# The second mixing one step later, a third buffer of mixed blocks, and the weight conversion spread over more steps

## The chip, the cores and the metric

The kernel runs on one core of a Trainium2 chip. The metric is the device time of one execution in microseconds (us), from start to end of the program. The profiler shows five engines: TensorE (PE, with its weight loads in a row of their own, PEld), VectorE (DVE), ScalarE (ACT), GpSimd (POOL) and SyncE (SP), which here issues DMAs.

## What is computed

Talking-heads attention (4 batches, 12 heads, 448 positions, 64 values a head), then a two-layer network on the result. Two 12x12 matrices mix the heads, one before and one after the softmax:

```python
scores = scale * np.matmul(q, k.transpose(0, 1, 3, 2))
scores = np.einsum('bhij,hg->bgij', scores, w_pre)
scores = scores - np.max(scores, axis=-1, keepdims=True)
attn = np.exp(scores)
attn = attn / (np.sum(attn, axis=-1, keepdims=True) + 1e-09)
attn = np.einsum('bhij,hg->bgij', attn, w_post)
out = np.matmul(attn, v).astype(np.float32)
...
h = x @ w_in
r = np.maximum(h, 0.0)
g = s * (r * r) + b
return (g @ w_out).astype(np.float32)
```

## The kernel before, in words

Precision is kept with pairs: a float32 value is split into a high and a low part, and a product takes three matmuls (low by high, high by low, high by high).

**Attention.** The query positions of a batch are cut into four chunks of 110, 110, 110 and 118 (`chunks`, 16 in all). For a chunk, `qk_pair` computes the scores of two heads (six matmuls, line 489) into the two PSUM banks of tag `sc`, and ScalarE copies them to `S` (line 499). DMAs lay `S` out again as blocks of ten positions by twelve heads on 120 partitions (`relayout`). There are 180 blocks: 11 to a chunk of 110, 12 to a chunk of 118. The main loop takes one block a step, in a software pipeline written out by hand. In step s, in this order:

- `split(s + 2)`: GpSimd splits a block into high and low (lines 563, 564);
- one operation of a weight conversion on VectorE (`convert_step`, steps 12 to 60), then `normalize(s - 1)`: reciprocal on VectorE (line 597) and the scaled block `eh` in float16 on ScalarE (line 599);
- `evacuate(s - 3)`: VectorE copies a mixed block from PSUM to `A` (line 637; in the last chunk ScalarE does it, line 635);
- `premix(s)`: the first mixing, three matmuls of 448 columns (line 578), the maximum on VectorE (line 580), the exponential and its sum on ScalarE (lines 585, 589). The result lies in one of three PSUM banks in turn;
- `remainder(s - 1)`: VectorE makes the float16 remainder of the normalized block into the second half of `eh` (line 606);
- `postmix(s - 2)`: the second mixing, twelve matmuls of 120 columns that load `eh` as weights (line 621), into one of two banks of tag `po`;
- what the plan gives the step: the scores of a later chunk (`qk_pair`), the product with V for an earlier one (`av_pair`, line 517, two heads, sixteen matmuls), transposes of q (`prep_q`, `trq`) and of k (`prep_k`, `trk`) into the `sc` banks, whose low parts VectorE makes at the next call of `low_parts` (line 232).

Each engine works through its own list in order. About every second step is given a `qk_pair` and an `av_pair` at once (steps 1, 3, 5, 7, 9 and the last of a chunk's window); the text calls these heavy, the others light. In a window of 11 steps the last two heavy ones adjoin; in one of 12 none do. ScalarE copies the products with V out of PSUM, `xs` (line 531), one or two copies after the fourth and after the sixth `av_pair` of a chunk (two in a chunk of 118).

The plan (`at`, `fill`, `run_plan`) is a list of step numbers. An `av_pair` of a chunk may begin at `first[ci + 1] + 3`, a step after the chunk's last block has been copied to `A`.

**Weight conversion.** The network's weights come as 64-bit floats. `conversion` turns one piece into a high and a low part by one ScalarE operation (line 153) and seven VectorE operations (lines 154 to 177); each call of `convert_step` does one VectorE operation of it. Seven pieces (`NU_EARLY`), 49 operations, are done during the attention, one a step from `CONV0 = 12`.

**Network.** From about 486 us on, two matrix products fill TensorE; the first pieces of the first (`head_piece`) are put into the attention's last steps as filling.

`keep` is a constant tile that feeds matmuls without use in the first steps (line 576), which only keep TensorE at work.

Of the kernel before, what the change touches and what calls it, by code (L numbers as in the profile page):

```python
# [11 lines left out]
F16 = mybir.dt.float16  # L12
# [9 lines left out]
def talking_heads_attention__then__act_relu2_kernel(  # L22
# [14 lines left out]
    B, H, S, D = q.shape  # L37
    DM = H * D
    DFF = moe_w_in.shape[1]
    P = 128  # L40
# [5 lines left out]
    NP = H // 2  # L46
    BI = 10
    BP = BI * H
# [13 lines left out]
    NCH = len(chunks)  # L62
# [3 lines left out]
    first = []  # L66
# [9 lines left out]
    NB = len(blocks)  # L76

    NU = 16
    NU_EARLY, NU_TAIL = 7, 6
# [6 lines left out]
    cvp = ctx.enter_context(tc.tile_pool(name="cvp", bufs=1))  # L86

    att = ExitStack()
    cst = att.enter_context(tc.tile_pool(name="cst", bufs=1))
    sp = att.enter_context(tc.tile_pool(name="sp", bufs=2))  # L90
    blkp = att.enter_context(tc.tile_pool(name="blkp", bufs=3))
# [90 lines left out]
    def convert_step(upto):  # L182

        if done["run"] is None:
            if done["conv"] >= min(upto, len(units)):
                return False
            done["run"] = conversion(done["conv"])
        try:
            next(done["run"])
        except StopIteration:  # L190
            done["run"] = None
            done["conv"] += 1
        return True
# [33 lines left out]
    later = []  # L227
# [4 lines left out]
            nc.vector.tensor_tensor(out=o, in0=x, in1=hi.bitcast(F32), op=ALU.subtract)  # L232

    banks = ["pm", "po", "pm", "po", "xp", "px"]
    turn = {"bank": 0}

    def bank(name):
        tag = banks[turn["bank"] % len(banks)]
# [301 lines left out]
    def qk_pair(ci, p):  # L540
        low_parts()
        for m in range(3):
            qk_part(ci, p, m)
# [7 lines left out]
    def relayout(t):  # L551
        ci, i0, ni = blocks[t]
        blk = blkp.tile([BP, S], F32, tag="blk", name=f"blk_{t}", bufs=LD)
        nb = first[ci + 1] - first[ci]
        r = t - first[ci]
        nc.sync.dma_start(blk[:ni * H, :], s_t[ci][r:r + nb * (ni - 1) + 1:nb, :, :])
        blk_t[t] = blk

    def split(t):
        n = blocks[t][2] * H  # L560
        blk = blk_t.pop(t)
        hl = blkp.tile([BP, 2, S], F32R, tag="hl", name=f"hl_{t}", bufs=2)
        nc.gpsimd.tensor_scalar(hl[:n, 0, :], blk[:n], 1.0, 0.0, op0=ALU.mult, op1=ALU.add)  # L563
        nc.gpsimd.tensor_tensor(  # L564
            out=hl[:n, 1, :], in0=blk[:n], in1=hl[:n, 0, :].bitcast(F32), op=ALU.subtract
        )
        hl_t[t] = hl
# [25 lines left out]
    def normalize(t):  # L593

        n = blocks[t][2] * H
        e, st = e_t[t]
        nc.vector.reciprocal(st[:n, 3:4], st[:n, 2:3])  # L597
        eh = blkp.tile([BP, 2, S], F16, tag="eh", name=f"eh_{t}", bufs=2)
        nc.scalar.activation(eh[:n, 0, :], e[:n], AF.Copy, scale=st[:n, 3:4])  # L599
        eh_t[t] = eh  # L600

# [9 lines left out]
    def postmix(t):  # L611
        ci, i0, ni = blocks[t]
        n = ni * H
        eh = eh_t.pop(t)
        if i0 == 0:
            a_t[ci] = ap_.tile([P, NC, H, CH], F32, tag="A", name=f"A_{ci}")
        po = ps.tile([P, 512], F32, tag="po", name=f"po_{t}", bufs=2)
        for c in range(NC):
            j0 = min(c * P, S - P)
            for m, (x, y) in enumerate(((1, 0), (0, 1), (0, 0))):  # L620
                nc.tensor.matmul(  # L621
                    po[:, c * BP:(c + 1) * BP],
                    eh[:n, x, j0:j0 + P],
                    wpost[:n, y].rearrange("p g i -> p (g i)"),
                    start=(m == 0),
                    stop=(m == 2),
                )
        po_t[t] = po

    def evacuate(t):  # L630
        ci, i0, ni = blocks[t]
        dst = a_t[ci][:, :, :, i0:i0 + ni]
        src = po_t.pop(t)[:, :NC * BP].rearrange("p (c g i) -> p c g i", c=NC, g=H)[:, :, :, :ni]
        if ci == NCH - 1:
            nc.scalar.activation(dst, src, AF.Copy)
        else:
            nc.vector.tensor_copy(dst, src)  # L637

    LD, LS = 5, 2
    CONV0 = 12  # L640
    FILL = 1.33
# [8 lines left out]
    def at(step, order, f, *args):  # L650
        plan.append((step, order, len(plan), f, args))
# [6 lines left out]
    def visits(ci):  # L658

        w0, w1 = first[ci - 1] - LD, first[ci] - LD  # L660
        return [w0 + i for i in (1, 3, 5, 7, 9, w1 - w0 - 1)]

    fill = []
    for ci in range(2, NCH):
        b, _, _ = chunks[ci]
        w0 = first[ci - 1] - LD
# [10 lines left out]
        for p, step in enumerate(visits(ci)):  # L677
            if news:
                t = w0 - back + 8 if p == 0 else w0 + 2 * p - 2
# [4 lines left out]
            load[step] = load.get(step, 0) + QK_COST  # L684
    for ci in range(NCH):
        b = chunks[ci][0]
        w0 = first[ci + 1] + 3
        if ci < NCH - 2:
            after = visits(ci + 3) if ci + 3 < NCH else [first[NCH - 1] - LD + i for i in (1, 3, 5, 7)]
            steps = [x for x in visits(ci + 2) if x >= w0] + [x for x in after if x < first[ci + 2] + 3]  # L690
            assert len(steps) == NP
            for p, step in enumerate(steps):
                at(step, 2, av_pair, ci, p)
                load[step] = load.get(step, 0) + AV_COST
                if b + 1 < B and chunks[ci + 1][0] != b:
                    at(step, 4, load_v, b + 1, p)
            continue
        w1 = first[ci + 2] + 3 if ci + 2 <= NCH else NB + 100
        if ci == NCH - 1:
            w0 = NB + 3  # L700
        for p in range(NP):
            when = w0 + p * min(w1 - w0, 12) / NP
            fill.append((when, w0, w1 - 1, AV_COST, 1, av_pair, (ci, p)))
    w0 = first[NCH - 1] - XA + 2
    for i in range(NHEAD * NKC):
        if i < NHEAD * NKC - LATE:
            j = i - (NHEAD * NKC - LATE - 4)
            if j < 0:
                when = w0 + i * (NB - 1 - w0) / (NHEAD * NKC - LATE - 4)
                fill.append((when, w0 + i // 2, NB + 2, 0.567, 1, head_piece, ()))  # L710
            else:
                at(NB - 1 + (0, 1, 1, 2)[j], 1, head_piece)
        else:
            fill.append((NB + 100, NB + 3, NB + 100, 0.567, 1, head_piece, ()))
    fill.sort(key=lambda x: x[0])
    spent, closed = 0.0, {}
    for s in range(NB + 4):
        spent = max(spent, -0.4) + load.get(s, 0)
        left, held = [], set()
        for x in fill:  # L720
            _, lo, hi, cost, order, f, args = x
            waits = f in held

            opens = f is qk_pair or (f is av_pair and args[1] % 4 == 0)
            if opens and closed.get(f, -1) >= s and s <= NB + 2 and s < hi:
                waits = True

            if f is qk_pair and s in load and s < hi:
                waits = True
            if not waits and lo <= s and (s > NB + 2 or hi <= s or (x[0] < s + 4 and spent < FILL)):  # L730
                at(s, order, f, *args)
                spent += cost
                if f is qk_pair or (f is av_pair and args[1] in (3, NP - 1)):
                    closed[f] = s
            else:
                held.add(f)
                left.append(x)
        fill = left
        spent -= FILL
# [12 lines left out]
        if not early:  # L752
            state["next"] = k0

    keep = cst.tile([P, 512], F16, name="keep")
    nc.gpsimd.memset(keep, 1.0)
    make_identity(nc, ident)
    busy = ps.tile([P, 512], F32, tag="px", name="busy")
# [51 lines left out]
    while plan[0][0] < 0:  # L810
        x = plan.pop(0)
        x[3](*x[4])
        low_parts()
    tail = first[NCH - 1]
    for s in range(NB + 3):
        if s == tail - LD:
            early.close()
            rp = ctx.enter_context(tc.tile_pool(name="rp", bufs=1, side="right", reuse_waits="tile"))
            for n in range(NU_EARLY, NU_EARLY + NU_TAIL):
                w_pool[n] = rp  # L820
        if s + LD < NB:
            relayout(s + LD)
        if s + LS < NB:
            split(s + LS)
        if 0 <= s - 1 < NB:
            if s >= CONV0:
                convert_step(NU_EARLY)
            normalize(s - 1)
        if 0 <= s - 3 < NB:
            evacuate(s - 3)  # L830
        if s <= tail - XA:
            low_parts()
        if s < NB:
            premix(s)
        low_parts()
        if s < 2:
            (build_scale, build_post)[s](*loaded_consts)
            qk_pair(1, NP - 2 + s)
        if 0 <= s - 1 < NB:
            remainder(s - 1)  # L840
        run_plan(s, True)
        if 0 <= s - 2 < NB:
            postmix(s - 2)
        run_plan(s, False)
        if 0 <= s - (tail - LD) < NKC // 2:
            for kc in range(2):
                load_x(0, 0, 2 * (s - (tail - LD)) + kc)
        if 0 <= s - (tail - XA) < NKC:
            split_x(0, 0, s - (tail - XA))
        if 0 <= s - tail < NKC:  # L850
            load_x(0, 1, s - tail)
# [107 lines left out]
```

## Time and profile before

| | |
|---|---|
| median of 3 executions | 961.35 us (959.28 to 961.48) |
| the profiled execution | 961.09 us, span in the trace 959.4 us |
| PE busy over the span | 929.8 us, 97% |
| PEld / DVE / ACT / POOL busy | 82% / 67% / 62% / 41% |
| chain that ended last, by engine | PE 64%, ACT 15%, DVE 13%, DMA 5% |
| granted TensorE clock | 1.00 of full speed (2.4 GHz) in nearly every slice |

A row of the waits names the engine that waited, the line that it waited in, the releaser, the time in total, how often and the longest. A row of the timeline gives start and duration in us, the engine, line and operation, and in brackets the idle time before it with its releaser. Matmuls are pipelined and their ends are modelled, so that a matmul's row can cover a part of the idle time behind it.

### The profile page before, as it was taken

To read this page: it belongs to the slowest core of one execution; us is meant where nothing else is said; L and a number is where in the kernel's file an instruction comes from. 1 tells how busy PE (TensorE), PEld (TensorE's weight loads), DVE (VectorE), ACT (ScalarE), POOL (GpSimd) and SP (SyncE) were. 2 spreads that over 40 slices of the span, in tenths; PEclk is the share of its full clock that TensorE was granted. 3 is DMA by queue.
4 is the path that set the end of the run, shared out by engine and by line. 5 is a ranking of instruction groups with operands and counts; after the bars stand their busy time and mean duration, and the time that the engine had idled before them with its cause. 6 is when DMAs were issued, how large, how long until landed. Compare 5 with 4: busy or idle time off the path is not lost.

```text
span 959.4 us, 19910 instructions
## 1 busy us (share of the span) xinstructions
PE 929.8 (97%) x7538; PEld 786.2 (82%) x7538; DVE 639.0 (67%) x1307; ACT 597.7 (62%) x1321; POOL 398.1 (41%) x469
## 2 busy tenths in 40 slices
PE   8899999999999999999999999999999999999998
PEld 4566767777777777777789999999998999999998
DVE  3899999888878888788678217656707711848311
ACT  5678778787888888877777977322216787711000
POOL 3866676666767667766613423100001332310000
PEclk9999999999999999999999999999999999999999
DMA  4665545654455544645323312245431410237431
GB/s 114 173 155 154 151 126 146 180 129 151 106 147 143 135 118 127 157 116 168 112 71 106 109 55 70 66 126 154 132 133 45 154 58 1 82 110 209 145 98 50
DMA packets 124252, 114.63 MB, mean 119 GB/s; under 512 B 61656, under 2 KB 120044, under 8 KB 124156
## 3 DMA queue, kind: packets, MB, share of 16 engines
q1 hardware_dynamic: 114630, 101.69, 38.3%
q10 hardware_dynamic: 9366, 11.59, 3.4%
q8 instruction: 59, 0.97, 0.4%
q14 instruction: 37, 0.30, 0.1%
q0 software_dynamic: 160, 0.09, 0.1%
HBM read 58.28 MB, written 16.52 MB: 78 GB/s over the span
## 4 chain that ended last, share of the span: by engine, by line
PE 64%; ACT 15%; DVE 13%; DMA 5%; issue 2%; POOL 0%; SPq 0%; ACTq 0%; DVEq 0%
PE po L300 24%; PE ph L247 17%; PE xp L517 6%; PE po L621 5%; ACT S L499 5%; PE sc L489 5%; PE pm L578 5%; ACT pm L585 4%; ACT eh L599 3%; DVE eh L606 3%; DVE A L637 2%; DVE st L580 2%; DMA raw<-in_moe_w_out_dram 2%; DMA nq<-in_q_dram 1%; PE trk L442 1%
## 5 line engine op out<-in xcount | busy, mean ns | idle before, releaser
L300 PE MATMUL po<-w,g 128*128 128x384 f32 x1344 | 234.6, 336 | 2.4 <-ACT h L255 2.4
L300 PEld LDWEIGHTS po<-w,g 128*128 128x128 f32 x1344 | 233.7, 188 | 3.1 <-ACT h L255 3.1
L564 POOL TENSOR_TENSOR hl<-blk,hl 120x448 fp32r<-120x448 f32 x180 | 206.0, 1145 | 15.0
L265 POOL TENSOR_TENSOR g<-h,g 128x448 fp32r<-128x448 f32 x64 | 77.9, 1217 | 287.9 <-ACT g L264 274.8
L621 PEld LDWEIGHTS <-eh 120*128 120x128 f16 (+1 forms) x2160 | 115.0, 98 | 63.4 <-DVE eh L606 40.5
L247 PE MATMUL ph<-x,w 128*128 128x448 f32 x810 | 166.2, 364 | 0.0
L247 PEld LDWEIGHTS ph<-x,w 128*128 128x128 f32 x810 | 152.0, 188 | 12.2
L563 POOL TENSOR_SCALAR hl<-blk 120x448 fp32r<-120x448 f32 x180 | 105.1, 584 | 136.2 <-PE pm L578 123.1
L621 PE MATMUL po<-wpost,eh 120*128 120x120 f16 (+1 forms) x2160 | 144.7, 217 | 14.6 <-DVE eh L606 14.1
L585 ACT ACTIVATE pm<-pm,st 120x448 f32<-120x448 f32 x180 | 109.8, 610 | 56.8 <-DVE st L580 56.2
L606 DVE SCALAR_TENSOR_TENSOR eh<-pm,st,eh 120x448 f16<-120x448 f32 x180 | 122.1, 679 | 16.6 <-ACT eh L599 13.2
L599 ACT ACTIVATE eh<-pm,st 120x448 f16<-120x448 f32 x180 | 114.1, 634 | 20.3 <-DVE st L597 17.2
L580 DVE TENSOR_REDUCE st<-pm 120x1 f32<-120x448 f32 x180 | 110.9, 616 | 22.0 <-PE pm L578 20.4
L637 DVE COPY A<-po 128x480 f32<-128x480 f32 x168 | 106.8, 635 | 0.0
L578 PE MATMUL pm<-hl,wpre_hi 120*120 120x448 f32 x360 | 101.9, 364 | 0.7 <-POOL hl L564 0.7
L153 ACT ACTIVATE mk<-raw 128x384 f32<-128x384 f32 x64 | 35.5, 554 | 93.7 <-DMA raw<-in_moe_w_out_dram 43.9
L517 PE MATMUL xp<-A,v 128*64 128x110 f32 (+1 forms) x1536 | 93.7, 265 | 0.0
L499 ACT ACTIVATE S<-sc 110x896 f32<-110x896 f32 (+1 forms) x91 | 83.3, 916 | 13.7 <-PE sc L489 11.5
L489 PE MATMUL sc<-Tk,Tq 64*110 64x448 f32 (+1 forms) x576 | 82.9, 393 | 2.3 <-ACT S L499 1.0
L578 PE MATMUL pm<-hl,wpre_lo 120*120 120x448 f32 x180 | 83.3, 463 | 0.1
L517 PEld LDWEIGHTS xp<-A,v 128*64 128x64 f32 x1536 | 74.2, 136 | 9.9 <-issue 1.2
L232 DVE TENSOR_TENSOR x<-xraw,x 128x448 fp32r<-128x448 f32 x36 | 23.9, 698 | 75.0 <-ACT x L223 75.0
(77 smaller groups left out, 1008.3 us busy)
## 6 DMA issues: line engine op xcount, KB each, us to landing
blk<-S SPq DMA_DIRECT2D x172, 210.0 KB
raw<-in_moe_w_in_dram SPq DMA_DIRECT2D x32, 384.0 KB
raw<-in_moe_w_out_dram SPq DMA_DIRECT2D x32, 384.0 KB
xraw<-xd SPq DMA_DIRECT2D x48, 224.0 KB
part<-ob ACTq DMA_DIRECT2D x28, 192.0 KB
acc<-part SPq DMA_DIRECT2D x28, 192.0 KB
out_dram<-acc ACTq DMA_DIRECT2D x28, 192.0 KB
v<-in_v_dram SPq DMA_DIRECT2D x24, 192.0 KB
```

The costliest lines, as they stand in the source:

```text
L247: nc.tensor.matmul(ph[:, :S], w[:, i, c0:c0 + P], x[:, y, :], start=(kc == 0 and m == 0), stop=(kc == NKC - 1 and m == 2),)
L300: nc.tensor.matmul(po[:, :NO], g[:, x, c0:c0 + P], w[:, y, :], start=(f == 0 and m == 0), stop=(f == NF - 1 and m == 2),)
L489: nc.tensor.matmul(sc[e][:n, :S], qt[r0:r0 + D, p, x, :n], kt[r0:r0 + D, y, :], start=(m == 0), stop=(m == 2),)
L499: nc.scalar.activation(s_t[ci][:n, 2 * p:2 * p + 2, :], x_t["two"][:n, :, :S], AF.Copy, scale=SCALE)
L517: nc.tensor.matmul(xp[e * D:(e + 1) * D, p % 4, :n], vt[:, e, c, :], a[:, c, 2 * p + e, :n], start=(c == 0), stop=(c == NC - 1),)
L564: nc.gpsimd.tensor_tensor(out=hl[:n, 1, :], in0=blk[:n], in1=hl[:n, 0, :].bitcast(F32), op=ALU.subtract)
L578: nc.tensor.matmul(pm[:n, :S], w[:n, :n], hl[:n, x, :], start=(m == 0), stop=(m == 2))
L580: nc.vector.tensor_reduce(out=st[:n, 0:1], in_=pm[:n, :S], axis=AX.X, op=ALU.max, negate=True)
L585: nc.scalar.activation(e[:n], e[:n], AF.Exp, bias=st[:n, 0:1], accum_out=pm[:n, S:S + 1])
L599: nc.scalar.activation(eh[:n, 0, :], e[:n], AF.Copy, scale=st[:n, 3:4])
L606: nc.vector.scalar_tensor_tensor(out=eh[:n, 1, :], in0=e[:n], scalar=st[:n, 3:4], in1=eh[:n, 0, :], op0=ALU.mult, op1=ALU.subtract,)
L621: nc.tensor.matmul(po[:, c * BP:(c + 1) * BP], eh[:n, x, j0:j0 + P], wpost[:n, y].rearrange("p g i -> p (g i)"), start=(m == 0), stop=(m = ...
```

## The change

`postmix` runs three steps behind `premix` in place of two, and `evacuate` four in place of three; `eh` has three buffers in place of two. The plan's step numbers that hang on it move by one (3 becomes 4), and the loop has one step more. The 49 conversion operations are no longer done one a step from step 12: an operation is done in a step when fewer than `49 * (s - 12) / 139` have been done and no low part is pending, which puts them at steps 13, 16, 18, 21 and so on to 149. `keep` moves into the buffer of the conversion's `mk`.

```diff
-    turn = {"bank": 0}
+    turn = {"bank": 0, "ops": 0}
...
-        eh = blkp.tile([BP, 2, S], F16, tag="eh", name=f"eh_{t}", bufs=2)
+        eh = blkp.tile([BP, 2, S], F16, tag="eh", name=f"eh_{t}", bufs=3)
...
-        w0 = first[ci + 1] + 3
+        w0 = first[ci + 1] + 4
         if ci < NCH - 2:
...
-            steps = [x for x in visits(ci + 2) if x >= w0] + [x for x in after if x < first[ci + 2] + 3]
+            steps = [x for x in visits(ci + 2) if x >= w0] + [x for x in after if x < first[ci + 2] + 4]
...
-        w1 = first[ci + 2] + 3 if ci + 2 <= NCH else NB + 100
+        w1 = first[ci + 2] + 4 if ci + 2 <= NCH else NB + 100
         if ci == NCH - 1:
-            w0 = NB + 3
+            w0 = NB + 4
...
-                at(NB - 1 + (0, 1, 1, 2)[j], 1, head_piece)
+                at(NB + (0, 1, 1, 2)[j], 1, head_piece)
...
-    keep = cst.tile([P, 512], F16, name="keep")
+    keep = cvp.tile([P, 6 * P], F16, tag="mk", name="keep")[:, :512]
...
-    for s in range(NB + 3):
+    for s in range(NB + 4):
...
         if 0 <= s - 1 < NB:
-            if s >= CONV0:
-                convert_step(NU_EARLY)
+            ops = 7 * NU_EARLY
+            if not later and turn["ops"] < ops * (s - CONV0) / (tail - LD - 2 * NP - CONV0):
+                turn["ops"] += convert_step(NU_EARLY)
             normalize(s - 1)
-        if 0 <= s - 3 < NB:
-            evacuate(s - 3)
+        if 0 <= s - 4 < NB:
+            evacuate(s - 4)
...
-        if 0 <= s - 2 < NB:
-            postmix(s - 2)
+        if 0 <= s - 3 < NB:
+            postmix(s - 3)
```

TensorE in a step in the middle of the attention (`pm_100` is the first mixing of block 100, `eh_98` the normalized block 98, `po_98` its second mixing). Before:

```order
L517 MATMUL xp_7_0_4540<-A_7_3937,v_1_3_2795 64x118 x8
L489 MATMUL sc_10_1_4772<-Tk_2_1_3647,Tq_10_4501 110x448 x6
L578 MATMUL pm_100_4793<-hl_100_4701,wpre_lo_126 120x448
L578 MATMUL pm_100_4793<-hl_100_4701,wpre_hi_125 120x448 x2
L621 LDWEIGHTS eh_98_4736
L621 MATMUL po_98_4802<-wpost_127,eh_98_4736 128x120
```

and now:

```order
L517 MATMUL xp_7_0_4492<-A_7_3928,v_1_3_2729 64x118 x8
L489 MATMUL sc_10_1_4726<-Tk_2_1_3586,Tq_10_4453 110x448 x6
L578 MATMUL pm_100_4748<-hl_100_4654,wpre_lo_126 120x448
L578 MATMUL pm_100_4748<-hl_100_4654,wpre_hi_125 120x448 x2
L621 LDWEIGHTS eh_97_4659
L621 MATMUL po_97_4757<-wpost_127,eh_97_4659 128x120
```

The second mixing at the same place is that of block 97; the products and scores beside it stand where they stood.

VectorE around steps 100 to 102 (`st` holds a block's maximum and reciprocal, `A` the mixed blocks of a chunk, `w`, `mk`, `u`, `raw` belong to a conversion). Before:

```order
L597 RECIPROCAL st_99_4743<-st_99_4743 120x1
L637 COPY A_8_4438<-po_97_4748 128x48x10
L580 TENSOR_REDUCE st_100_4797<-pm_100_4793 120x1
L606 SCALAR_TENSOR_TENSOR eh_99_4790<-pm_99_4739,st_99_4743,eh_99_4790 120x448
L597 RECIPROCAL st_100_4797<-st_100_4797 120x1
L637 COPY A_8_4438<-po_98_4802 128x48x10
```

and now:

```order
L167 SCALAR_TENSOR_TENSOR w_4_4372<-mk_4_4373,u_4_4374 128x384
L597 RECIPROCAL st_99_4697<-st_99_4697 120x1
L637 COPY A_8_4439<-po_96_4702 128x48x10
L580 TENSOR_REDUCE st_100_4752<-pm_100_4748 120x1
L606 SCALAR_TENSOR_TENSOR eh_99_4745<-pm_99_4693,st_99_4697,eh_99_4745 120x448
L597 RECIPROCAL st_100_4752<-st_100_4752 120x1
L637 COPY A_8_4439<-po_97_4757 128x48x10
```

The copies to `A` are a block later, the remainders (line 606) are not, and a conversion operation stands ahead of a reciprocal where none stood. At step 20 it is the other way: before, each step has one.

## Rows read from the trace of the kernel before

**Rows 1.** Busy time by stretch: steps 12 to 60, then steps 61 to 148.

```profile
core 0: us, PE busy (x) PEld busy (x) DVE busy (x) ACT busy (x) POOL busy (x), PEclk, DMA share, GB/s
53.10:182.90 129.80, 123.18 (x1347) 89.69 (x1345) 120.58 (x261) 102.21 (x255) 89.04 (x106) 1.00 0.55 147
182.90:405.50 222.60, 218.72 (x2449) 162.32 (x2448) 182.99 (x382) 180.24 (x450) 151.13 (x189) 1.00 0.51 136
```

**Rows 2.** The same stretches, line 578 alone (three matmuls a step; PE, then PEld).

```profile
53.10:182.90 129.80, 42.43 (x147) 22.90 (x147) 1.00 0.55 147
182.90:405.50 222.60, 75.89 (x265) 41.24 (x266) 1.00 0.51 136
```

**Rows 3.** TensorE's waits, five stretches in order: from 23.7, 53.1, 182.9, 405.5, 451.9 us.

```profile
PE po L621 <- DVE eh L606: 3.0, 5, 1.5
...
PE po L621 <- DVE eh L606: 4.5, 13, 1.0
PE trq L464 <- ACT S L499: 0.9, 4, 0.3
...
PE po L621 <- DVE eh L606: 3.4, 18, 0.3
...
PE po L621 <- DVE eh L606: 1.9, 8, 0.5
...
PE po L621 <- DVE eh L606: 1.3, 2, 0.9
```

**Rows 4.** Timeline of a light step (from 299.65 us) and the heavy one behind it.

```profile
299.65 0.47 PE L578 MATMUL pm<-hl,wpre_lo 120*120 120x448 f32 x1
...
300.36 0.80 PE L621 MATMUL po<-wpost,eh 120*128 120x120 f16 x12
...
300.58 0.63 ACT L599 ACTIVATE eh<-pm,st 120x448 f16<-120x448 f32 x1
...
300.97 0.44 PE L578 MATMUL pm<-hl,wpre_lo 120*120 120x448 f32 x1
...
301.21 0.61 ACT L585 ACTIVATE pm<-pm,st 120x448 f32<-120x448 f32 x1
301.24 0.68 DVE L606 SCALAR_TENSOR_TENSOR eh<-pm,st,eh 120x448 f16<-120x448 f32 x1
...
301.98 0.80 PE L621 MATMUL po<-wpost,eh 120*128 120x120 f16 x12 [0.15 <-DVE eh L606]
...
302.20 0.64 DVE L637 COPY A<-po 128x480 f32<-128x480 f32 x1
...
302.75 0.61 DVE L580 TENSOR_REDUCE st<-pm 120x1 f32<-120x448 f32 x1
...
303.40 0.61 ACT L585 ACTIVATE pm<-pm,st 120x448 f32<-120x448 f32 x1 [0.39 <-DVE st L580]
...
304.11 0.17 ACT L589 ACTIVATE st<-pm 120x1 f32<-120x1 f32 x1
...
304.39 0.64 DVE L637 COPY A<-po 128x480 f32<-128x480 f32 x1
...
304.53 0.92 ACT L499 ACTIVATE S<-sc 118x896 f32<-118x896 f32 x1 [0.25 <-PE sc L489]
...
305.34 0.63 ACT L599 ACTIVATE eh<-pm,st 120x448 f16<-120x448 f32 x1
```

**Rows 5.** The chain of waits, two adjoining steps (first mixing: start, duration).

```profile
211.09 0.80 PE pm L578 x3
...
214.24 0.80 PE pm L578 x3
...
216.22 0.80 PE pm L578 x3
```

**Rows 6.** Groups of instructions: longest and shortest conversion operation on VectorE; the xs copies.

```profile
L158 DVE SCALAR_TENSOR_TENSOR u<-raw,u 128x384 uint32<-128x384 uint32 x64 | 39.9, 623 | 2.0
...
L154 DVE TENSOR_SCALAR u<-raw 128x384 uint32<-128x384 uint32 x64 | 26.3, 412 | 6.3 <-DMA raw<-in_moe_w_out_dram 4.4 <-DMA raw<-in_moe_w_in_dram 0.5
...
L531 ACT ACTIVATE xs<-xp,xscale 128x440 f32<-128x440 f32 (+5 forms) x40 | 18.5, 485 | 3.5 <-PE xp L517 3.5
```

More of the change, by code (lines that the diff above doesn't have):

```diff
@@ L709, in talking_heads_attention__then__act_relu2_kernel @@
                 when = w0 + i * (NB - 1 - w0) / (NHEAD * NKC - LATE - 4)
-                fill.append((when, w0 + i // 2, NB + 2, 0.567, 1, head_piece, ()))
+                fill.append((when, w0 + i // 2, NB + 3, 0.567, 1, head_piece, ()))
             else:
-                at(NB - 1 + (0, 1, 1, 2)[j], 1, head_piece)
+                at(NB + (0, 1, 1, 2)[j], 1, head_piece)
         else:
-            fill.append((NB + 100, NB + 3, NB + 100, 0.567, 1, head_piece, ()))
+            fill.append((NB + 100, NB + 4, NB + 100, 0.567, 1, head_piece, ()))
     fill.sort(key=lambda x: x[0])
     spent, closed = 0.0, {}
-    for s in range(NB + 4):
+    for s in range(NB + 5):
         spent = max(spent, -0.4) + load.get(s, 0)
@@ L724, in talking_heads_attention__then__act_relu2_kernel @@
             opens = f is qk_pair or (f is av_pair and args[1] % 4 == 0)
-            if opens and closed.get(f, -1) >= s and s <= NB + 2 and s < hi:
+            if opens and closed.get(f, -1) >= s and s <= NB + 3 and s < hi:
                 waits = True
@@ L729, in talking_heads_attention__then__act_relu2_kernel @@
                 waits = True
-            if not waits and lo <= s and (s > NB + 2 or hi <= s or (x[0] < s + 4 and spent < FILL)):
+            if not waits and lo <= s and (s > NB + 3 or hi <= s or (x[0] < s + 4 and spent < FILL)):
                 at(s, order, f, *args)
```

## The prediction

> **What bounds the kernel now.** I read the busy time by stretch first, because the change lies wholly in the attention (the first 486 us); the network behind it keeps its order and its operations, so I give it no difference. In steps 61 to 148 TensorE is busy for 218.72 of 222.60 us, and in steps 12 to 60 for 123.18 of 129.80, where VectorE is busy for 120.58 [rows 1]. The clock was granted in full in both. The first mixing's matmuls, three to a step, count the steps: 147 and 265, so 49 and 88.3 [rows 2]. A step takes 2.65 us in the first stretch and 2.52 in the second; the 0.13 between them is what the conversions are worth where they now stand, in all ways together.
>
> Next, what TensorE waited for. Nearly all of its idle time in the attention stands at one place: the second mixing, waiting for VectorE's remainder of the block (line 606): 3.0, 4.5, 3.4, 1.9 and 1.3 us in the five stretches, 14.1 us in 46 waits [rows 3].
>
> The timeline shows why [rows 4]. In the light step the first mixing starts at 299.65 and the second at 300.36, 0.71 behind it: no wait. In the heavy step they start at 300.97 and 301.98, 1.01 apart: 0.30 lost, of which the row shows 0.15, as a matmul's modelled end covers the rest. What TensorE waits for there has come down a chain: the copy of scores to S on ScalarE, behind it in the same list the scaled block (300.58), then the remainder on VectorE (301.24), then the second mixing. The next pair repeats it: S at 304.53, the scaled block 0.81 later. So a heavy step's S stands ahead of the block that the next heavy step's second mixing needs. The light step took 1.32 us; a heavy one without a wait takes 3.15 (211.09 to 214.24, all of it in the chain on TensorE) and a light one with a transpose of k 1.98 [rows 5].
>
> **What the change does, and what each part costs.** No engine gets or loses an instruction. On TensorE each step keeps its products and scores; only the block of the second mixing is an older one. SP's and GpSimd's work keeps its place against the first mixing.
>
> *Gain 1: the waits at line 621.* With three steps of distance the remainder that the second mixing needs was made one step earlier, at least 1.32 us before; the longest of the 41 waits behind step 11 shows 1.0 us. They go. Their price is the 11.1 us shown behind 53.1 us plus 0.15 hidden in each of 41, 6.15: 17.25 us. The five in steps 0 to 11 (3.0 + 0.75 = 3.75 us) I count at 0.5: there TensorE has next to nothing but the mixings, and VectorE and ScalarE go round in a loop of their own (below), so that what TensorE no longer waits for here, it waits for at the next block. Bounds 0 and 3.75.
>
> *Gain 2: conversions leave steps 13 to 60.* 32 of 49 go. The 0.13 us a step above are 6.3 us in 49 steps. Part of it is already in gain 1: the waits there cost 4.5 + 13 x 0.15 = 6.45, or 0.13 a step, against (3.4 + 18 x 0.15)/88.3 = 0.07 in the other stretch, so 0.06 x 49 = 3.1. The rest is 3.2; 32/49 of it is 2.1 us. Bounds 0 and 3.2.
>
> *What takes over.* Once TensorE no longer waits, the next loop is that of VectorE and ScalarE, which the distance does not touch: copy to A, maximum, exponential, sum, reciprocal, copy to A. A whole turn without a wait for TensorE is 302.20 to 304.39, 2.19 us [rows 4]. In a heavy step ScalarE's own list is the longer way: exponential to sum 0.71, sum 0.17, S to scaled block 0.81, scaled block to the next exponential 0.63 (300.58 to 301.21): 2.32. A light and a heavy step together take 4.51 on this loop and 1.32 + 3.15 = 4.47 on TensorE. They are level, so everything that is added to the loop counts.
>
> *Cost 1: the conversions on the loop.* From the start of the maximum (302.75) to the next copy to A (304.39) VectorE has 1.64 us, of which maximum and remainder take 0.61 + 0.68; 0.35 are left. The seven operations take between 0.41 and 0.62 [rows 6], 0.55 in the mean: 0.20 too much. In a heavy step ScalarE's way is the longer one and hides most of it, so half of the 49 count: 4.9 us. By the plan one light step in five also has a transpose of k, whose 0.66 us on TensorE hides it: 4 us. Bounds 0 (all covered) and 49 x 0.20 = 9.8.
>
> *Cost 2: the xs copies.* They stand in ScalarE's list ahead of S, 0.485 us each, 40 in all [rows 6]. Until now ScalarE had waits there to fill (0.39 and 0.25 in the two steps shown); on the loop they count. In an 11-step chunk two copies, 0.97, meet one pair of adjoining heavy steps with 3.15 - 2.32 = 0.83 to spare, and I leave that out. A 12-step chunk has four copies and no such pair: 1.94 us, three times before the last chunk: 5.8. Bounds 0 and 18.5, all of them.
>
> *Edits that I cost at nothing.* The third buffer: its release is a step away as before. The first product with V of a chunk still stands in the same steps; only the slack behind the copy to A shrinks from two steps to one, and a step is over twice the copy's 0.64. `keep` in the buffer of `mk`: the first conversion operation now waits for a matmul of the step before, which is long done. The step added at the end: its head pieces fill TensorE as they did; if they did not, one second mixing, 0.65 us, would stand bare.
>
> *Sum.* 17.25 + 0.5 + 2.1 - 4 - 5.8 = 10.05 us. Against the profiled execution's own 961.1 us (span 959.4) that is 951.0. The median of the runs, 961.35, lies 0.26 above the profiled one, which I leave aside: **951 us**, with 945 to 957 for this case by the bounds of the two costs at half their width.
>
> **The rivals.**
>
> *TensorE alone binds.* Lags on the loop can be made up, since three PSUM banks let the first mixing run ahead, and both costs vanish: 14.1 + 46 x 0.15 = 21.0, and 2.1: 23.1 us, 938 (935 to 944). For it: around 211 us the chain runs through TensorE alone over adjoining steps [rows 5]. Against it: the two loops are level there only because transposes of k lengthen TensorE's way.
>
> *The loop binds, and the wait only moves.* It comes back where TensorE wants the `sc` banks for a transpose while ScalarE is still copying S (0.9 us in four waits already [rows 3]) or a bank of the first mixing. The costs at their bounds, 9.8 and 18.5, are more than gain 1, so that nothing of it is left, and gain 2 (2.1 to 3.2) remains: 958 (955 to 962). For it: VectorE busy for 93% of steps 12 to 60 [rows 1]. Against it: TensorE busy for 98% of steps 61 to 148, with VectorE at 82%.
>
> The Trainium skill has a rule on this side (Perfetto Trace Analysis, Identifying the Most-Contended Engine): TensorE's headroom is judged by its weight loads, not by matmul busy time, and the engine with the highest occupancy is to be relieved first. By that rule steps 12 to 60, with weight loads at 69% and VectorE at 93%, are VectorE's; taking a wait from TensorE would give nothing there, and the time would be this rival's 958. The trace bears the rule out in part: there, but not in the longer stretch.
>
> *Slower: the conversions find no gap in their new steps.* Place: the 32 operations that come into steps 61 to 149, where VectorE had none, each ahead of a reciprocal. If VectorE runs late there, the 0.35 us gap is gone and each costs its whole 0.55, 17.6 us, half of it in light steps, 8.8. On top of the rival above that is 958 + 8.8 = 967. It decides when an operation costs more than about 0.1 us each on the path (3.2/32) and the lost waits return nothing.
>
> That the change does not do what it says is no rival: the order shows both moves on their engines.
>
> **How the numbers follow.** A measurement of this kernel can tell about 0.3%, 2.9 us, from no change. Chances: the forecast 0.53, TensorE alone 0.21, the loop 0.20, slower 0.06. Faster by over 0.3% (under 958.5): 0.52 of the forecast, 0.21, half of the loop's 0.10: 0.83. Within 0.3%: 0.01 + 0.10 = 0.11. Slower: 0.06. The range from 938 to 959 leaves out the lower third of the second case (0.07), what of the third lies above 959 (0.07) and the last (0.06).
>
> **What would show it.** Right: the row of line 621 waiting for line 606 all but gone from TensorE's waits; pairs of a light and a heavy step at 4.5 us in place of 4.77 (4.47 + 0.30); steps 13 to 60 at 2.5 us or less; VectorE waiting less for the sum (line 589) and more of the chain on ScalarE and VectorE. Wrong on cost 1: light steps with a conversion as short as those without. Wrong altogether: new waits at the transposes, at line 578 or at line 517 that add up to more than 10 us, or TensorE's stretch from 182.9 us longer than 222.6.

## The result, and the profile after

The changed kernel takes 949.54 us (median of 4 executions, 948.54 to 951.14), the kernel before, in the same series, 960.40 (959.28 to 961.48): a ratio of 0.9889, 95% interval 0.9868 to 0.9909, or 10.9 us. 951 was forecast, in a range from 938 to 959.

The busy time by stretch of the changed kernel, for steps 12 to 60, then 61 to 149:

```profile
core 0: us, PE busy (x) PEld busy (x) DVE busy (x) ACT busy (x) POOL busy (x), PEclk, DMA share, GB/s
51.00:174.50 123.50, 120.32 (x1346) 89.73 (x1346) 107.18 (x229) 99.75 (x251) 86.78 (x106) 1.00 0.54 142
174.50:397.20 222.70, 218.39 (x2466) 163.78 (x2465) 193.88 (x415) 181.20 (x456) 152.90 (x190) 1.00 0.53 142
```

The second stretch of [rows 1] ends one step earlier, after 222.60 us. Up to the end of step 149 the kernel before takes 223.98:

```profile
182.90:406.88 223.98, 220.10 (x2467) 163.47 (x2466) 183.89 (x383) 181.62 (x452) 151.76 (x191) 1.00 0.51 136
```

VectorE has 13 us less in the first stretch and 10 more in the second. The first is 6 us shorter; the second, which won at the second mixing and lost elsewhere, only 1.2. TensorE's waits over the whole execution, which answer to [rows 3]:

```profile
PE trq L464 <- ACT S L499: 7.3, 16, 1.4
PE po L300 <- ACT h L255: 2.5, 2, 1.3
PE pm L576 <- DVE eh L606: 1.8, 2, 1.5
...
PE po L621 <- ACT A L635: 1.4, 3, 0.6
```

The row "L621 <- DVE eh L606", 14.1 us in 46 waits, is gone. At the head stands one that was 0.9 us in four waits: the transposes of q, which want an `sc` bank while ScalarE still copies S out of it. The row of line 576 is new too: in the first steps TensorE now waits for the same remainder at the next block's first matmul (29.80 and 37.52 us). The timeline shows a pair without a wait and, one pair on, how that new wait comes about:

```profile
236.01 0.47 PE L578 MATMUL pm<-hl,wpre_lo 120*120 120x448 f32 x1
...
237.33 0.44 PE L578 MATMUL pm<-hl,wpre_lo 120*120 120x448 f32 x1
...
238.02 0.80 PE L621 MATMUL po<-wpost,eh 120*128 120x120 f16 x12
...
240.44 0.47 PE L578 MATMUL pm<-hl,wpre_lo 120*120 120x448 f32 x1
...
244.08 0.86 PE L489 MATMUL sc<-Tk,Tq 64*110 64x448 f32 x6
...
244.70 0.61 ACT L585 ACTIVATE pm<-pm,st 108x448 f32<-108x448 f32 x1 [0.39 <-DVE st L580]
...
245.40 0.17 ACT L589 ACTIVATE st<-pm 108x1 f32<-108x1 f32 x1
245.47 0.63 ACT L531 ACTIVATE xs<-xp,xscale 128x440 f32<-128x440 f32 x1
...
245.59 0.81 PE L621 MATMUL po<-wpost,eh 120*128 120x120 f16 x12
...
245.99 0.91 ACT L499 ACTIVATE S<-sc 110x896 f32<-110x896 f32 x1
...
246.96 0.41 PE L464 MATMUL trq<-ident,nq 110*128 110x110 f32 x2 [0.56 <-ACT S L499]
```

The light step is 1.32 us and the heavy one behind it 3.11, 4.43 together, with the second mixing 0.69 behind the first. Later the scores end at 244.94, but ScalarE has the exponential, its sum and an xs copy ahead of S in its list, begins S at 245.99 and copies until 246.90; the transposes, which could have followed the second mixing of 245.59, wait for that.

To see where the time went I took the start of the first mixing in each step from the timeline and measured stretches between them, in us:

```
stretch                             before   changed   difference
start to step 0                      23.70     21.92      -1.78
steps 0 to 11                        29.44     29.04      -0.40
steps 12 to 60                      129.78    123.53      -6.25
steps 61 to 149                     223.98    222.74      -1.24
steps 150 to 167                     45.00     42.09      -2.91
step 168 to the network's own
  first matmul (494.62 / 481.87)     42.72     42.55      -0.17
the network                         464.78    464.93      +0.15
span                                959.40    946.80     -12.60
```

The first line is no effect of the change (last section); without it 10.8 us are left, close to the 10.9 of the medians. For steps 13 to 167, the time over the shortest step of the same kind (3.13 us heavy, 1.66 and 1.48 with four and two transposes of q, 1.98 with transposes of k), summed, with the runs that follow:

```
                              80 heavy steps   44 light steps with transposes
before                             16.4                 6.3
changed                             1.4                13.2
distance alone                      2.6                14.9
spread alone                       16.5                 4.6
changed, no conversion              1.1                 9.2
changed, scores first              32.2                 2.8
changed, xs in the next step        5.9                 4.1
```

So 15 us went from the heavy steps, and 7 came back in the light ones with transposes. The remaining 31 steps (28 light ones without a transpose and three with only one of the two products) lost 2.3 us.

### The profile page after: what moved, and what is told of

It is laid out like the page before. It is cut to its first block, busy times and chain, and to the rows that moved or that the text cites. A ratio compares the mean times of both kernels' runs of the same rounds, so it can differ in the third digit from the quotient of the medians.

```text
span 946.8 us, 20022 instructions
## 1 busy us (share of the span) xinstructions
PE 921.6 (97%) x7538; PEld 786.5 (83%) x7538; DVE 634.0 (67%) x1307; ACT 594.3 (63%) x1321; POOL 397.5 (42%) x469
## 4 chain that ended last, share of the span: by engine, by line
PE 67%; ACT 14%; DVE 11%; DMA 6%; issue 1%; POOL 0%; ACTq 0%; SPq 0%; DVEq 0%; POOLq 0%
PE po L300 24%; PE ph L247 17%; PE pm L578 7%; PE po L621 6%; PE xp L517 5%; PE sc L489 4%; ACT pm L585 4%; ACT S L499 4%; DMA blk<-S 4%; ACT eh L599 2%; DVE A L637 2%; DVE st L580 2%; PE trk L442 1%; PE ph_head L247 1%; DMA nq<-in_q_dram 1%
## 5 line engine op out<-in xcount | busy, mean ns | idle before, releaser
L621 PEld LDWEIGHTS <-eh 120*128 120x128 f16 (+1 forms) x2160 | 115.3, 98 | 40.8 <-issue 40.6
L621 PE MATMUL po<-wpost,eh 120*128 120x120 f16 (+1 forms) x2160 | 144.6, 217 | 1.4 <-ACT A L635 1.4
L606 DVE SCALAR_TENSOR_TENSOR eh<-pm,st,eh 120x448 f16<-120x448 f32 x180 | 122.2, 679 | 24.9 <-ACT eh L599 21.6
```

The source lines that it names most:

```text
L606: nc.vector.scalar_tensor_tensor(out=eh[:n, 1, :], in0=e[:n], scalar=st[:n, 3:4], in1=eh[:n, 0, :], op0=ALU.mult, op1=ALU.subtract,)
L621: nc.tensor.matmul(po[:, c * BP:(c + 1) * BP], eh[:n, x, j0:j0 + P], wpost[:n, y].rearrange("p g i -> p (g i)"), start=(m == 0), stop=(m = ...
```

## The experiments

Every run was timed against the kernel before on its own chip; ratios are to that.

**The distance alone.** The conversion goes back to one operation a step:

```diff
-            ops = 7 * NU_EARLY
-            if not later and turn["ops"] < ops * (s - CONV0) / (tail - LD - 2 * NP - CONV0):
-                turn["ops"] += convert_step(NU_EARLY)
+            if s >= CONV0:
+                convert_step(NU_EARLY)
```

> The changed kernel, but with the conversion as before: one operation a step from step 12 to 60. Theory (the distance gives the gain, and conversions cost time on the loop of VectorE and ScalarE wherever they stand): heavy steps without a wait as in the changed kernel (3.15 us); steps 12 to 60 lose most of what they won, in the light steps with transposes; steps 61 to 149 gain about 3 us against the changed kernel. Together 950 to 953 us, 8 to 10 us below the kernel before. Rival (the spreading gives the gain of steps 13 to 60): 955 us or more.

Measured: 953.32 us, ratio 0.9933 (0.9921 to 0.9946), 6.4 us below before: 0.3 us above the expected time and a smaller gain than expected, yet below the rival's 955. Its heavy steps have hardly any waits (2.6 us over the shortest in 80 steps). Steps 12 to 60 take 128.61 us, 1.2 less than before: there the distance alone returned nearly nothing, with VectorE busy for 118.18 of 128.70 us: the heavy steps of that stretch won about 5 us, those with transposes lost about 4.5:

```profile
52.00:180.70 128.70, 120.99 (x1345) 89.95 (x1345) 118.18 (x261) 101.94 (x254) 89.77 (x108) 1.00 0.56 149
...
PE trq L464 <- ACT S L499: 8.1, 14, 1.5
```

Steps 61 to 149 take 220.49, 3.5 less than before and 2.3 less than in the changed kernel.

**The spread alone.** The kernel before with the changed kernel's three lines for the conversion.

> The kernel before, with only the conversion spread as in the change: distance two, two buffers. Theory: heavy steps keep their waits at line 621 (14 us in 46 waits shown before); steps 13 to 60 gain 2 to 3 us, steps 61 to 149 lose as much: 958 to 962 us. Rival (the spreading gives the gain): 955 us or less.

Measured: 956.36 us, ratio 0.9967 (0.9954 to 0.9979), 3.2 us below before. Both were missed: the theory by 2 us, the rival by 1. The waits at line 621 stand as they stood:

```profile
PE po L621 <- DVE eh L606: 13.4, 44, 1.5
```

Steps 12 to 60 take 125.85 (3.9 less than before), steps 61 to 149 226.00 (2.0 more). The operations cost less where they go than where they were, so the spread is a gain by itself. The two parts, 6.4 and 3.2 us, add up to 9.6 of the 10.9, which the intervals do not tell from all of it.

**No conversions.** For the first seven pieces GpSimd writes zeros:

```diff
+        if n < NU_EARLY:
+            for i in range(2):
+                nc.gpsimd.memset(w[:, i, :].bitcast(F32), 0.0)
+                yield
+            for i in range(4):
+                yield
+            load_raw()
+            return
```

> The changed kernel without the 49 conversion operations and their seven operations on ScalarE: GpSimd writes zeros for the first seven pieces instead, in the same steps; the loads stay. The output leaves these weights out. Theory (cost 1: an operation of conversion costs about 0.1 us on the loop of VectorE and ScalarE, 4 us together): 945 to 947 us, with shorter light steps where a transpose stands. Rival (TensorE alone binds and the conversions are covered): 949 to 950 us, no change.

Measured: 945.99 us, ratio 0.9858 (0.9843 to 0.9873), 3.5 us below the changed kernel (3.0 by the ratios), as the theory said. Steps 12 to 60 take 121.79 (1.74 less than changed, for 17 operations), steps 61 to 149 220.21 (2.53 less, for 32): 0.10 and 0.08 us an operation, 4.3 together. The seven ScalarE operations of the conversion go with them, so this is the price of both engines' part. Of the 4.3, 4.0 came back in the steps with transposes (3.3 with those of q); the 21 light steps without a transpose in steps 13 to 149 take 27.80 us with the conversions and without. Done one a step, in the run with the distance alone, 49 operations cost 128.61 - 121.79 = 6.8, or 0.14 each. The transposes still wait for S (line numbers are eight higher in this kernel):

```profile
PE trq L472 <- ACT S L507: 4.4, 11, 1.3
```

**Scores first.** In each heavy step the scores come ahead of the product with V:

```diff
-            at(step, 3, qk_pair, ci, p)
+            at(step, 1.5, qk_pair, ci, p)
```

> The changed kernel with the scores ahead of the product with V in each heavy step, so that ScalarE copies S before the xs copies and the sc banks come free earlier. Theory (what is left is TensorE's transposes waiting for ScalarE's copy of S, pushed back by xs: 13 us over the shortest in steps 13 to 167, 7.3 us of it shown as waits): the waits at line 464 shrink to under 3 us, 944 to 947 us. Rival (the loop of VectorE and ScalarE is late as a whole, whatever the order of its copies): 948 to 951 us, the wait in the transposes goes to another place.

Measured: 970.16 us, ratio 1.0115 (1.0097 to 1.0132). A miss for both times. The transposes' wait fell to 2.0 us and their steps to near the shortest, as the theory said, but each heavy step became 0.4 us longer. Waits, then the timeline of one place:

```profile
PE sc L489 <- DVE Tq L232: 23.7, 28, 1.4
PE sc L489 <- DVE Tk L232: 5.6, 19, 0.6
PE trq L464 <- ACT S L499: 2.0, 4, 1.3
...
299.42 0.64 DVE L232 TENSOR_TENSOR Tq<-trq,Tq 128x472 fp32r<-128x472 f32 x1
...
300.12 0.87 PE L489 MATMUL sc<-Tk,Tq 64*110 64x448 f32 x6 [1.22 <-DVE Tq L232]
```

A transpose's result lies in the same banks as the scores, and VectorE reads it there for the low part. The transposes shown are of a chunk of 118 (472 columns for four), the scores behind them of a chunk of 110: what these wait for is the banks, not the data. With the product with V first, its 0.9 us on TensorE cover that reading; with the scores first they wait for it. So the order of the two is no free choice: the `sc` banks make the transposes wait for S in one order and the scores wait for the transposes in the other.

**The last chunk's copies on VectorE.**

```diff
-        if ci == NCH - 1:
-            nc.scalar.activation(dst, src, AF.Copy)
-        else:
-            nc.vector.tensor_copy(dst, src)
+        nc.vector.tensor_copy(dst, src)
```

> The changed kernel with the last chunk's copies to A (line 635) on VectorE in place of ScalarE. In the changed kernel the second mixing of the last steps waits for these copies (1.4 us shown in three waits, some 0.15 hidden in each). Theory (this is a new wait that the greater distance brought in, and gives back part of what steps 168 to 178 won): the three waits go, 947 to 948 us, 1 to 2 us below the changed kernel. Rival (the last block's chain sets the end whatever engine copies): no change.

Measured: 949.79 us, ratio 0.9900 (0.9883 to 0.9916): no change from the changed kernel. The rival holds. In the changed kernel the second mixing of the last steps waits for ScalarE's copies, and here for VectorE's (first fence changed, second this run):

```profile
465.59 0.79 PE L621 MATMUL po<-wpost,eh 120*128 120x120 f16 x12 [0.28 <-ACT A L635]
...
467.74 0.79 PE L621 MATMUL po<-wpost,eh 120*128 120x120 f16 x12 [0.45 <-ACT A L635]
...
469.83 0.79 PE L621 MATMUL po<-wpost,eh 108*128 108x120 f16 x12 [0.63 <-ACT A L635]
```

```profile
469.87 0.79 PE L621 MATMUL po<-wpost,eh 120*128 120x120 f16 x12 [0.26 <-DVE A L634]
...
472.06 0.79 PE L621 MATMUL po<-wpost,eh 108*128 108x120 f16 x12 [0.73 <-DVE A L634]
```

From step 179 to the network's first matmul it takes 16.94 us against 17.39, less than a median tells.

**The xs copies in the next step.** `av_part` keeps the copies and their DMA in a list, which is worked off behind the next step's `premix`, or at once where the next step has a product with V:

```diff
+            xs_later.append(copies)
+            s1 = turn.get("step", NB + 200) + 1
+            if s1 >= NB or any(x[0] == s1 and x[3] is av_pair for x in plan):
+                flush_xs()
...
+        turn["step"] = s
         if s < NB:
             premix(s)
+        flush_xs()
```

> The changed kernel with the xs copies moved in ScalarE's list from ahead of S to behind the sum of the next step, except where the next step has a product with V. Theory (cost 2: the xs copies stand on the loop in heavy steps, and push S and so the transposes back; a light step has room for them): the excess of the light steps with transposes of q, 13 us with those of k in the changed kernel, falls by 4 to 6 us, 944 to 946 us. Rival (the loop is late by its own 2.19 and 2.32 us; an xs copy costs the same wherever it stands): 949 to 950 us.

Measured: 946.64 us, ratio 0.9865 (0.9849 to 0.9881): a gain of 2.9 us (2.3 by the ratios), a little under the theory's; the time is well off the rival's. The two runs side by side below tell the gain better. The excess of the steps with transposes fell from 13.2 to 4.1, more than expected, and heavy steps got 4.5 back, since the next product with V waits for the xs copy to free its bank:

```profile
PE xp L517 <- ACT xs L532: 3.2, 11, 0.5
PE trq L464 <- ACT S L499: 2.4, 6, 1.3
```

**The third buffer alone.**

```diff
-        eh = blkp.tile([BP, 2, S], F16, tag="eh", name=f"eh_{t}", bufs=2)
+        eh = blkp.tile([BP, 2, S], F16, tag="eh", name=f"eh_{t}", bufs=3)
...
-    keep = cst.tile([P, 512], F16, name="keep")
+    keep = cvp.tile([P, 6 * P], F16, tag="mk", name="keep")[:, :512]
```

> The kernel before with only the third buffer of mixed blocks and the constant tile in the conversion's buffer; distance two, one conversion operation a step. Theory (the distance counts, not the buffer): 959 to 961 us, no change from before; at most the 1.8 us go in which ScalarE's scaled block waited for the second mixing. Rival (the buffer alone lets the chain run ahead): 957 us or less.

Measured: 960.89 us, ratio 1.0007 (0.9998 to 1.0016). The theory holds: the buffer does nothing without the distance. Whether the distance would do without the buffer was not run.

**Both edits together** (xs in the next step, the last chunk's copies on VectorE).

> Both edits of the two runs before on the changed kernel: xs copies behind the next step's sum, and the last chunk's copies to A on VectorE. Theory: their gains add, 942 to 945 us. Rival: 947 us or more.

Measured: 947.28 us, ratio 0.9864 (0.9849 to 0.9879). The rival's time holds: the expectation fell with that of the copies on VectorE, and nothing is added to the xs edit.

**The changed kernel and the xs edit side by side,** on one chip.

> The changed kernel as it is, beside the next run on the same chip. Theory: 949 to 951 us, ratio to before 0.988 to 0.991. Its steps 12 to 167 take 388 us within 1 us; where its time in a profile differs from the first by more, the difference stands ahead of step 0, where the first transposes take 0.7 or 1.1 us each four.

> The changed kernel with the xs copies behind the next step's sum, beside the changed kernel on the same chip. Theory: steps 12 to 167 4 us shorter than in the changed kernel, the median 3 to 5 us below it. Rival (the 3 us seen between two jobs were the chips'): within 1 us of it.

Measured: 949.28 us, ratio 0.9887 (0.9870 to 0.9904), and 946.19 us, ratio 0.9854 (0.9838 to 0.9871): 3.1 us apart. Steps 12 to 167 take 388.36 and 384.33 us in the two profiles. All of this is as expected, and the rival, that the gain lay in the chips, falls. The version with the xs copies in the next step beats the changed kernel, and both beat the kernel before.

## Why the prediction was right

*Gain 1, the waits at line 621 (17.25 us behind step 11).* Right in mechanism and in size: the row is gone, and the steps without transposes lost 17.3 us in steps 13 to 167, 15.0 of it in heavy ones. Part of the agreement is luck. The 38 waits in them show 9.5 us, so if all of the 17.3 was theirs, 0.20 lay hidden in each and not 0.15; and the two waits in the last stretch (1.3 us shown, 0.3 hidden) did not come back: the second mixing there waits for the copies to A instead, and step 168 to the network takes 42.55 us against 42.72. I had costed the end at nothing, and missed that a wait of its own would turn up there. The third buffer alone returns nothing.

*Steps 0 to 11 (0.5 us).* 0.40 measured. There the loop of VectorE and ScalarE goes on as before, and TensorE waits for it one block later (the row of line 576).

*Gain 2, conversions leaving steps 13 to 60 (2.1 us, at most 3.2).* The prediction means their price in the kernel before, outside the waits of gain 1, and the run with the spread alone measures that: steps 12 to 60 are 3.9 us shorter, 1.9 of it in steps without transposes, where the waits at line 621 stand, and 2.0 in those with transposes. With the distance in, the same move returns more: 128.61 us against 123.53, or 5.1, for an operation in every step then costs 0.14 us and one in three 0.10. That 5.1 can't be added to cost 1 below, which has the conversions' new price already.

*Cost 1, the conversions on the loop (4 us).* 4.3 measured by taking them away: right in size, wrong in place. I charged the light steps and let those with a transpose of k hide it. The light steps without a transpose show nothing (27.80 us either way); 3.3 us of the price stand in steps with transposes of q and 0.7 in those with transposes of k.

*Cost 2, the xs copies (5.8 us).* The mechanism is shown: moving the copies takes 9.1 us off the steps with transposes, and 4.0 to 4.4 us net off steps 12 to 167. The place was not as I put it. I charged only the chunks with four copies and let adjoining heavy steps make up for the others; of the 9.1 us, 2.6 come in the windows of the plan in which four are copied and 6.3 in those with two. TensorE does not wait for the loop as a whole, but where a transpose, above all one of q, comes next behind an xs copy and S. That 5.8 lies between the net and the whole effect is luck.

*The sum.* It closes for the right reason in the large. The steps without transposes won 17.3 us, against 15.65 forecast for the 39 waits of steps 12 to 167; those with transposes lost 6.9, against 7.7 (4 + 5.8 - 2.1); the start and the end gave 0.6, against 2.1. With the network's 0.15 that is 10.8 us, against 10.05. How the 7.7 was shared out among the steps was wrong in both costs.

*The signs.* The lost row, the pairs of a light and a heavy step (4.43 us) and VectorE's shorter wait for the sum (24.0 us, 31.3 before) came as said, and TensorE's new waits at transposes, 7 us, stayed under 10. Steps 13 to 60 take 2.54 us each, just over the 2.5 named. One sign failed: the chain that ended last did not move to ScalarE and VectorE (14% and 11% of the span, 15% and 13% before) but to TensorE (67%, 64% before).

*The rivals.* "TensorE alone binds" falls: taking the conversions away or moving the xs copies each makes the kernel 3 us shorter. "The loop binds, and the wait only moves" named the right place for the new wait, the `sc` banks, and is right for steps 12 to 60 if the conversions stay there: the distance alone returned 1.2 us of 129.78. The rule of the Trainium skill (Perfetto Trace Analysis, Identifying the Most-Contended Engine), to relieve the engine with the highest occupancy first, with TensorE judged by its weight loads, agrees with the trace there, with VectorE at 118.18 of 128.70 us and weight loads at 89.95. From step 61 on VectorE is ahead of the weight loads too [rows 1], yet the distance returned 3.5 us in steps 61 to 149: there the trace does not bear it out. "Slower" falls: an operation costs 0.08 us in its new steps, not 0.55.

Left open: taking the conversions away removes 4.0 of the 13.2 us of excess in the steps with transposes, moving the xs copies 9.1, each with the other in place. Together that would be nearly all of it, but no run has both, so what part the low parts have is not shown.

## What to carry to other kernels

A wait at one instruction in every second step, behind a chain over two other engines, is a matter of distance: put the consumer one step later with one more buffer, and price it by the step's length with and without the wait, since the wait's row shows only a part of it (here 9.5 us of 17.3). Then look at what is level with the engine that was freed, because small copies there, in an in-order list ahead of the one that frees a bank, can now set the pace; here putting them into the next step was worth 3 us more. Filler work was cheaper spread out here: an operation in each step cost 0.14 us, one in three 0.10.

## What the runs showed of the hardware that was not expected

Before step 0 the profiles differ by up to 2.6 us without any change of the program there. In the kernel before, and in four of the ten experiments, four transposes of k near 7 us take 1.14 us; in the changed kernel 0.70. The first fence is the kernel before, the second the changed one:

```profile
6.70 1.14 PE L442 MATMUL trk<-ident,A_k 128*128 128x128 f32 x4
```

```profile
6.49 0.70 PE L442 MATMUL trk<-ident,A_k 128*128 128x128 f32 x4
```

Step 0 begins at 23.7 to 24.3 us where these transposes take 1.14, and at 21.7 to 22.3 where they and the next ones take 0.70. The kernel with the xs copies in the next step has shown both (24.14 and 22.30). This accounts for 1.8 of the 12.6 us between the two profiled executions.

The granted clock goes with it, although the profile shows it as 1.00 from 6.3 to 10.3 us in both kernels. The records of the granted clock begin only at 9.90 us in the trace of the kernel before, at 5.18 in that of the changed one, and a stretch ahead of the first record is shown as 1.00. The run with the third buffer alone has its first record at 4.88 us, and there the clock changes between two groups of transposes:

```profile
4.95:8.20 3.25, 1.57 (x12) 0.92 (x11) 0.35 (x1) 2.20 (x3) 0.95 (x2) 1.00 0.76 194
8.35:11.60 3.25, 3.25 (x15) 2.20 (x14) 1.29 (x3) 1.07 (x3) 1.22 (x3) 0.50 0.68 167
...
7.08 0.69 PE L442 MATMUL trk<-ident,A_k 128*128 128x128 f32 x4
8.42 1.14 PE L442 MATMUL trk<-ident,A_k 128*128 128x128 f32 x4
```

Four transposes take 0.69 us at the full clock (2.4 GHz) and 1.14 at the half (1.2 GHz). TensorE was busy for 1.57 of 3.25 us before the clock fell and for all of 3.25 before it rose again. In the six executions where step 0 begins late, the records have the full clock from 9.90 to 11.71 us on; in the six others from 4.65 to 6.02. Why it comes at one time or the other no run here shows.
